# Softmax weights times values in float16 halves in the third and fourth token tile

## The chip, the cores and the metric

The kernel runs on one core of a Trainium2 chip. The metric is the device time of one execution in microseconds (us), lower is better. The kernel before takes 804.23 us, the median of 3 runs (804.05 to 804.49).

## The reference

```python
    x = A_x
    xn = _layernorm(x, axis=-1)
    s = _A_ref(xn, A_wqkv, A_wo)
    g = _silu(_B_ref(xn, B_w1, B_w3, B_w2))
    return x + s * g
...
        H = 32; Dh = D // H; W = 256
        qkv = (lambda x, *d: x.transpose(*d))((x @ wqkv).reshape(B, S, 3, H, Dh), 2, 0, 3, 1, 4)
        q, k, v = qkv[0], qkv[1], qkv[2]
        scores = jnp.einsum("bhqd,bhkd->bhqk", q, k) * (Dh ** -0.5)
        mask = (idx[:, None] - idx[None, :] >= 0) & (idx[:, None] - idx[None, :] < W)
        scores = jnp.where(mask[None, None], scores, -1e9)
        p = _softmax(scores, axis=-1)
        o = jnp.einsum("bhqk,bhkd->bhqd", p, v)
        return (lambda x, *d: x.transpose(*d))(o, 0, 2, 1, 3).reshape(B, S, D) @ wo
...
        gate = jnp.einsum("bsd,df->bsf", x, w1)
        up = jnp.einsum("bsd,df->bsf", x, w3)
        h = _silu(gate) * up
        out = jnp.einsum("bsf,fd->bsd", h, w2)
```

2048 tokens of 512 features go through a layernorm. Branch A is attention with 32 heads of 16 features, in which a token sees itself and the 255 tokens before it; branch B is a gated feed-forward layer of width 1792. All of it is in float32.

## The kernel before

**Halves.** Most products go through TensorE as float16: each operand is the sum of a high half (the number rounded to float16) and a low half (what the rounding left), and three products are summed: high times high, high times low, low times high. One product is an exception: the softmax weights times the values (L787) go through TensorE in float32, as one product.

**Tiles and units.** The 2048 tokens are cut into four token tiles of 512 (`t`, 0 to 3), the heads into four groups of eight (`g`). A unit is four of a group's eight heads in one token tile (`p`, 0 or 1): 32 units, numbered in order, so 16 to 31 belong to the third and fourth token tile. Each unit goes through two passes. `pass1` (L653) finds the maximum of each row of scores: eight pieces of matmuls (L671), each followed by two VectorE reductions with the window's mask (L685); then the maxima are negated (L704, L705), turned by a small matmul, copied (L717) and sent by DMA into rows of the query operand, so that the scores of pass 2 come out with the maximum subtracted. `pass2` (L738) computes the scores again, keys on the partitions, in five chunks of 128 x 1024 (L759); VectorE adds the masks (L766); ScalarE takes the exponential into a float32 tile `pt` (L769); and when all five are there, the values are multiplied in one burst (L787) of 48 float32 products, each of 64 rows (keys) by 32 columns (values of one head, with a column of ones that sums the weights), at eight places of the array. VectorE copies the result `po` out of PSUM (L802, L803), and units later it is normalised and multiplied by `wo`. While the chunks of a unit run, `pass1` of a later unit runs between them.

**Values.** `value(j)` (L553) projects the values of 128 tokens; ScalarE writes them with a scale to block `j % 10` of the tile `V`, float32, 17 columns for a head, the last of them ones.

**What else runs.** Between these pieces the dense products are spread: gate and up (L1055; ScalarE's sigmoid L1070, VectorE's products L1074 and L1079, and the casts and subtractions that make halves, L1110 to L1113), the projections of q and k (L601; L618 on ScalarE, L622 on VectorE), the folded down projection (L1198, L1280), and the output (L1332; L1326 on ScalarE, L1327 and L1336 on VectorE). L339 and L343 to L345 are helpers for the halves.

**Order.** Only TensorE runs in the order in which the code is written (`ORDERED`). That order comes from `batches`: a plan for each unit says which rows of work go into one batch, W being the scores of one chunk, M, X and N pieces of row maxima (X takes the bank `po`, N is narrow), the digits the chunks whose values are multiplied; `spread` lays dense work between the batches. The other engines are ordered by the scheduler of the language: each engine's instructions form one queue that is worked off in order, and `urgent()` puts an instruction ahead in it.

**Buffers.** PSUM has two banks `m` for dense results, two double banks `s` for scores and maxima, and one double bank `po`. SBUF has 54 slots (`take` and `give`) of 2 KB a partition; the exponentials have five buffers of their own (`pt`, from `ppool`).

```python
    PLAN = (("WM", ()), ("WMX", ()), ("WMX", ()), ("WWX", ()), ("NN", (0, 1, 2, 3, 4)))
```

## Time and profile before

| | |
|---|---|
| runs (3) | 804.23 us median, 804.05 to 804.49 |
| the profiled execution | 803.54 us, of which its span is 801.4 us |
| busy: TensorE, its weight loads | 791.6 us (99% of the span), 404.0 us (50%) |
| busy: VectorE, ScalarE, GpSimd | 620.4 us (77%), 395.5 us (49%), 387.6 us (48%) |
| clock granted to TensorE | full in every slice of the span |
| costliest on TensorE | L1055 first product 267.3 us in 896 instructions; L787 77.2 us in 2880 |
| costliest on VectorE | L685 133.9 us in 276 instructions out of `s` and 83.4 us in 172 out of `po`; L766 118.8 us in 280 |
| costliest on ScalarE | L769 167.6 us in 152 instructions |

A time of a group is the time in which at least one of its instructions ran, so groups whose instructions overlap share time. Busy is what the engine worked; the span is from the first to the last instruction, and 2.1 us of the execution lie around it. In the windows that follow, TensorE's clock, the share of the DMA engines and GB/s stand at the end of a row. In the timelines a row is the start, the duration, the engine, the line and operation, what it writes and reads, and in brackets how long the engine had been idle and what released it.

### The profile page before, as it was taken

How to read it: one execution, taken by the hardware profiler on the slowest of the kernel's cores; microseconds unless marked ns; L12 is line 12 of the kernel's file. 1: busy time of each engine (PE TensorE's matmuls, PEld its weight loads, DVE VectorE, ACT ScalarE, POOL GpSimd, SP SyncE). 2: the span in 40 equal slices, each digit the busy share in tenths (PEclk: the TensorE clock that was granted, in tenths of full speed). 3: DMA queues.
4: the chain of work that ended last, by engine and by line, in shares of the span. 5: the costliest groups of instructions: out<-in, count | busy, mean ns of one | idle time of the engine just before them, and what ended most of it. 6: DMA issues, size and time to landing. Idle time of an engine off the chain costs nothing.

```text
span 801.4 us, 23995 instructions
## 1 busy us (share of the span) xinstructions
PE 791.6 (99%) x9181; PEld 404.0 (50%) x9181; DVE 620.4 (77%) x2001; ACT 395.5 (49%) x596; POOL 387.6 (48%) x762
## 2 busy tenths in 40 slices
PE   9999999999999999999999999999999999999997
PEld 4444445444454444444445444466544744467465
DVE  8886889778798678787888887776678876874537
ACT  6989777744355544344443344344434334444411
POOL 2357657633329436365443546330446276650770
PEclk9999999999999999999999999999999999999999
DMA  9887655636666564657556743656553553343431
GB/s 284 239 260 239 202 185 145 242 111 193 189 216 187 168 212 139 212 156 255 142 191 171 209 115 101 180 169 159 140 158 90 156 161 106 89 121 127 133 89 60
DMA packets 109858, 134.18 MB, mean 167 GB/s; under 512 B 18928, under 2 KB 64944, under 8 KB 109744
## 3 DMA queue, kind: packets, MB, share of 16 engines
q1 hardware_dynamic: 109456, 132.13, 55.4%
q8 instruction: 72, 1.18, 0.7%
q10 hardware_dynamic: 288, 0.52, 0.2%
q14 instruction: 42, 0.34, 0.1%
HBM read 91.23 MB, written 36.57 MB: 159 GB/s over the span
## 4 chain that ended last, share of the span: by engine, by line
PE 81%; DVE 6%; DMA 5%; ACT 3%; SPq 3%; issue 1%; POOL 1%; DVEq 0%; ACTq 0%; POOLq 0%
PE m L1055 31%; PE po L787 9%; PE m L601 8%; PE m L1198 8%; PE m L1280 7%; PE s L759 5%; PE m L1332 4%; PE m L567 4%; PE s L671 3%; DMA slot<-in_B_w_dram 2%; PE po L671 2%; DVE junk L685 1%; POOL slot L345 1%; DMA KA<-dK 1%; SPq L880 1%
## 5 line engine op out<-in xcount | busy, mean ns | idle before, releaser
L1055 PE MATMUL m<-XH,slot 128*128 128x512 f16 x896 | 267.3, 380 | 0.8 <-DVE slot L1074 0.4
L769 ACT ACTIVATE pt<-s,es 128x1024 f32<-128x1024 f32 x152 | 167.6, 1113 | 175.9 <-DVE s L766 168.8
L1055 PEld LDWEIGHTS <-slot 128*128 128x128 f16 x1344 | 124.8, 98 | 155.2 <-issue 12.6
L1055 PE MATMUL m<-XL,slot 128*128 128x512 f16 x448 | 169.8, 379 | 0.0
L766 DVE TENSOR_TENSOR s<-s,MK 128x256 f32<-128x256 f32 (+2 forms) x280 | 118.8, 434 | 54.5 <-PE s L759 50.0
L685 DVE CUSTOM_DVE_ANT_0 junk<-s,MW 128x320 bf16<-128x320 f32 x276 | 133.9, 485 | 19.8 <-PE s L671 11.3
L339 POOL TENSOR_TENSOR slot<-slot,slot 128x256 f16<-128x256 f32 (+1 forms) x86 | 57.6, 693 | 121.4 <-DVE slot L1336 54.7
L345 POOL TENSOR_TENSOR slot<-slot,slot 128x128 f16<-128x128 f32 x184 | 74.9, 441 | 77.8 <-ACT slot L343 51.3
L685 DVE CUSTOM_DVE_ANT_0 junk<-po,MW 128x320 bf16<-128x320 f32 x172 | 83.4, 485 | 4.6
L1280 PE MATMUL m<-slot,slot 128*128 128x512 f16 x336 | 78.5, 380 | 1.4 <-DVE slot L1074 1.4
L787 PE MATMUL po<-pt,V 64*32 64x320 f32 (+4 forms) x2880 | 77.2, 342 | 0.1
L601 PE MATMUL m<-XH,slot 128*128 128x512 f16 x240 | 70.8, 380 | 0.5 <-DVE slot L1074 0.5
L1198 PE MATMUL m<-slot,slot 128*128 128x256 f16 x588 | 68.4, 273 | 0.0
L1070 ACT ACTIVATE slot<-m,sgs 128x512 f32<-128x512 f32 x56 | 38.3, 685 | 60.4 <-PE m L1055 60.3
L1113 POOL TENSOR_TENSOR slot<-slot,slot 128x256 f16<-128x256 f32 x98 | 64.6, 671 | 1.1
L1198 PEld LDWEIGHTS <-slot 128*128 128x128 f16 x588 | 56.2, 98 | 11.4 <-issue 2.8
L787 PEld LDWEIGHTS po<-pt,V 64*32 64x32 f32 x2880 | 50.5, 106 | 22.4 <-issue 0.8
L1074 DVE SCALAR_TENSOR_TENSOR slot<-slot,m 128x512 f32<-128x512 f32 x56 | 38.3, 684 | 28.4 <-ACT slot L1070 27.9
L759 PE MATMUL s<-qa,KA 50*64 50x320 f16 (+3 forms) x1472 | 58.3, 259 | 0.0
L601 PEld LDWEIGHTS <-slot 128*128 128x128 f16 x392 | 36.5, 98 | 42.6 <-issue 1.8
L759 PEld LDWEIGHTS <-KA 50*64 50x64 f16 x1472 | 30.1, 105 | 51.7 <-issue 31.5
L1280 PEld LDWEIGHTS <-slot 128*128 128x128 f16 x336 | 30.8, 98 | 39.5 <-issue 5.1
(194 smaller groups left out, 1132.6 us busy)
## 6 DMA issues: line engine op xcount, KB each, us to landing
slot<-dW SPq DMA_DIRECT2D x98, 256.0 KB
slot<-in_B_w_dram SPq DMA_DIRECT2D x56, 256.0 KB
slot<-dFold SPq DMA_DIRECT2D x48, 256.0 KB
dW<-slot SPq DMA_DIRECT2D x42, 256.0 KB
slot<-in_A_x_dram SPq DMA_DIRECT2D x30, 256.0 KB
KA<-dK SPq DMA_DIRECT2D x24, 288.0 KB
slot<-dWQ SPq DMA_DIRECT2D x24, 256.0 KB
qa<-dQ SPq DMA_DIRECT2D x30, 192.0 KB
```

The source lines that it names most:

```text
L339: op(out[:, c], a[:, c], b[:, c])
L345: nc.gpsimd.tensor_sub(lo[:, c:c + P], raw[:, c:c + P], hi[:, c:c + P])
L601: nc.tensor.matmul(cell["pp"][:, cols[n]], w[:, (a * NC + c) * P:(a * NC + c + 1) * P], b[:, c, cols[n]], start=n == 0 and (c, i) == parts ...
L685: lasts["maximum"] = nc.vector.tensor_tensor_reduce(out=junk[:, :n], in0=s[:, r, :n], in1=mask, scale=1.0, scalar=NEG, op0=ALU.add, op1=AL ...
L759: nc.tensor.matmul(s[64 * h:64 * h + 64, r, o:o + 64 * n], ka[rows, 2 * p + a, 64 * (m + 4):64 * (m + 5)], qa[rows, 2 * p + a, 64 * (m + k ...
L766: nc.vector.tensor_add(v, v, MK[:, kind, of:of + n, :].unsqueeze(1).to_broadcast([P, 2 * len(which), n, 64]))
L769: lasts["exp"] = nc.scalar.activation(pt, s, AF.Exp, scale=es)
L787: nc.tensor.matmul(cell["po"][32 * i:32 * i + 32, h, 64 * (m + k):64 * (m + k + n)], V[64 * h:64 * h + 64, (4 * t + m // 2) % VB, hd * VW: ...
L1055: nc.tensor.matmul(cell[k], w[:, (a * NC + c) * P:(a * NC + c + 1) * P], b[:, c, :], start=c == 0 and i == 0, stop=c == NC - 1 and i == 2)
L1113: nc.gpsimd.tensor_sub(lo, view, hi)
L1198: nc.tensor.matmul(cell["ps"][:, c], made[:, f:f + P], wj[:, g:g + 256], start=j == j0 and c == 0 and n == 0, stop=j == j1 - 1 and n == 2, ...
L1280: nc.tensor.matmul(ps, hh[:, a * TW + b * P:a * TW + (b + 1) * P], w[:, c * D:(c + 1) * D], start=f == f0 and i == 0, stop=f == f1 - 1 and ...
```

## The change

For the tiles `t` = 2 and 3 (units 16 to 31) the weights and the values become float16 halves, and the burst becomes three products of 48 matmuls each, 144 in all, in the order high weights by high values, high weights by low values, low weights by high values, within each group of pieces. The first two tiles keep the float32 product.

For each chunk of such a unit, the exponential (L790 now) is written to one of two float32 tiles, `pt0` and `pt1` in turn; ScalarE copies it to the high half (L801, 1024 columns); VectorE subtracts the high half from the second 512 columns (L802) and GpSimd from the first 512 in two pieces of 256 (L804). The halves of chunks 0 and 1 lie in slots, those of chunks 2, 3 and 4 in the buffers `pt2` to `pt4`. `urgent()` stands around all of these.

The values of blocks 8 to 15 are written as two halves (ScalarE the high one, a new VectorE operation the low one, four GpSimd memsets the columns of ones and the rest); blocks 6 and 7, which the second and the third tile read, are split by `part_values` at unit 13. The scale of the values becomes a constant, so two small scales that were computed at the start fall away. The plan of the two tiles is `PARTED_PLAN`: two chunks of scores in the first batch, in place of the fourth, and the first piece of maxima is in the second batch; units 30 and 31 keep `LAST_PLANS`. `parted` lets the matmul that turns the earlier unit's maxima go after the first piece of maxima of a unit.

```diff
--- before.py
+++ after.py
@@ -50,6 +50,8 @@
 TWO_ONES = struct.unpack("f", struct.pack("ee", ONE, ONE))[0]
 VW = DH + 1
 VB = 10
+VS = 2.0**8
+VR = H * VW + DH
 SLOTS = 54
 ORDERED = {ENGINE.PE}
 GROUPS = ((0, 4), (4, 8), (8, 11), (11, 14))
...
@@ -219,7 +222,9 @@
     for nm in NM:
         nc.gpsimd.memset(nm, 0.0)
 
-    V = const.tile([P, VB, H * VW + DH], F32, name="V")
+    V = const.tile([P, VB, VR], F32, name="V")
+    VF = {}
+    in_pt = [0]
     KA = [const.tile([P, 4, KW], F16, name=f"KA{r}") for r in range(3)]
     dQ = [dram.tile([P, TERMS, S], F16, name=f"dQ{g}") for g in range(NG)]
     dK = [dram.tile([P, TERMS, S], F16, name=f"dK{g}") for g in range(NG)]
@@ -565,10 +570,24 @@
             for c in (2 * half, 2 * half + 1):
                 for i, (a, b) in enumerate(((xh, WVH), (xh, WVL), (xl, WVH))):
                     nc.tensor.matmul(pv, a[:, c, tok], b[c], start=c == 0 and i == 0, stop=c == NC - 1 and i == 2)
-            if half:
+            if not half:
+                return
+            by_head = lambda v: v[:, 0:H * VW].rearrange("p (h w) -> p h w", w=VW)
+            pv = pv.rearrange("p (h d) -> p h d", d=DH)
+            s = VS / (WS * XS)
+            if j < 8:
                 with urgent():
-                    nc.scalar.activation(V[:, j % VB, 0:H * VW].rearrange("p (h w) -> p h w", w=VW)[:, :, 0:DH],
-                                         pv.rearrange("p (h d) -> p h d", d=DH), AF.Copy, scale=sc["uv"])
+                    nc.scalar.activation(by_head(V[:, j % VB, :])[:, :, 0:DH], pv, AF.Copy, scale=s)
+                return
+            both = V[:, j % VB, :].bitcast(F16)
+            VF[j] = hi, lo = both[:, 0:VR], both[:, VR:]
+            with urgent():
+                nc.scalar.activation(by_head(hi)[:, :, 0:DH], pv, AF.Copy, scale=s)
+                lasts["emptied"] = nc.vector.scalar_tensor_tensor(by_head(lo)[:, :, 0:DH], pv, s, by_head(hi)[:, :, 0:DH],
+                                                                  op0=ALU.mult, op1=ALU.subtract)
+            for v, one in ((hi, VS / OS), (lo, 0.0)):
+                nc.gpsimd.memset(by_head(v)[:, :, DH], one)
+                nc.gpsimd.memset(v[:, H * VW:], 0.0)
         return opening([(6, lambda h=h: part(h)) for h in range(2)])
 
 
@@ -673,12 +692,12 @@
             after = []
             if narrow:
                 pass
-            elif alone[0] and maxima and (ii, a) != (0, 0):
+            elif alone[0] and maxima and (parted[0] or (ii, a) != (0, 0)):
                 after = [f(s) for f in maxima]
                 maxima.clear()
             elif alone[0] and besides:
                 after = [besides.pop(0)(s)]
-            alone[0] = not after or t * NG + g <= 2
+            alone[0] = not after or t * NG + g <= 2 or parted[0]
             for r in range(2):
                 junk = ppool.tile([P, D], BF16, name="junk", bufs=1)
                 with urgent():
@@ -764,9 +783,25 @@
                 v = sv[:, :, first:first + by * (n - 1) + 1:by, :]
                 with urgent():
                     nc.vector.tensor_add(v, v, MK[:, kind, of:of + n, :].unsqueeze(1).to_broadcast([P, 2 * len(which), n, 64]))
-            cell[c] = pt = ppool.tile([P, 2, 512], F32, name="pt")
+            if t < 2:
+                in_pt[0] += 1
+            pt = ppool.tile([P, 2, 512], F32, name="pt", tag=f"pt{c % 2 if t > 1 else in_pt[0] % 5}", bufs=1)
             with urgent():
                 lasts["exp"] = nc.scalar.activation(pt, s, AF.Exp, scale=es)
+            if t < 2:
+                cell[c] = pt
+                return
+            if c < 2:
+                cell[c] = hi, lo = [take(F16) for _ in range(2)]
+            else:
+                both = ppool.tile([P, 2048], F16, name="pt", tag=f"pt{c}", bufs=1)
+                cell[c] = hi, lo = both[:, 0:1024], both[:, 1024:]
+            pt = pt.rearrange("p r q -> p (r q)")
+            with urgent():
+                lasts["exp"] = nc.scalar.copy(hi, pt)
+                nc.vector.tensor_sub(lo[:, 512:], pt[:, 512:], hi[:, 512:])
+                for q in (0, 256):
+                    nc.gpsimd.tensor_sub(lo[:, q:q + 256], pt[:, q:q + 256], hi[:, q:q + 256])
 
         begun = set()
 
@@ -779,7 +814,23 @@
                 for item in pieces(c):
                     if item[3][4]:
                         turns.setdefault(item[1:3], []).append((c, *item))
-            for group in zip_longest(*(turns[k] for k in sorted(turns))):
+            groups = list(zip_longest(*(turns[k] for k in sorted(turns))))
+            if t > 1:
+                for group in groups:
+                    for kv, kp in ((0, 0), (1, 0), (0, 1)):
+                        for c, o, h, a, (m, k, n, _, _) in filter(None, group):
+                            for r in range(2):
+                                i = 2 * r + a
+                                hd = g * 8 + r * 4 + 2 * p + a
+                                nc.tensor.matmul(cell["po"][32 * i:32 * i + 32, h, 64 * (m + k):64 * (m + k + n)],
+                                                 VF[4 * t + m // 2][kv][64 * h:64 * h + 64, hd * VW:hd * VW + 32],
+                                                 cell[c][kp][64 * h:64 * h + 64, 512 * r + o:512 * r + o + 64 * n],
+                                                 start=(h, i) not in begun, stop=c == len(chunks) - 1 and kp == 1,
+                                                 skip_group_check=True)
+                                begun.add((h, i))
+                give(*cell[0], *cell[1], after=2)
+                return
+            for group in groups:
                 for c, o, h, a, (m, k, n, _, _) in filter(None, group):
                     for r in range(2):
                         i = 2 * r + a
@@ -1469,6 +1520,7 @@
     FIRST_PLAN = (("WM", ()), ("WMX", ()), ("WMX", ()), ("WMX", ()), ("M", (0, 1, 2, 3)))
     PLAN = (("WM", ()), ("WMX", ()), ("WMX", ()), ("WWX", ()), ("NN", (0, 1, 2, 3, 4)))
     AHEAD_PLAN = (("MMX", ()), ("MMX", ()), ("MM", ()))
+    PARTED_PLAN = (("WW", ()), ("WMX", ()), ("WMX", ()), ("WMX", ()), ("NN", (0, 1, 2, 3, 4)))
     LAST_PLANS = ((("LW", ()), ("WW", ()), ("WW", ()), ("", (0, 1, 2, 3, 4))),
                   (("WW", ()), ("WW", ()), ("W", ()), ("", (0, 1, 2, 3, 4))))
 
@@ -1476,7 +1528,7 @@
 
         rows1 = pass1(*ahead) if ahead else []
         rows2, cols = pass2(*u) if u else ([], None)
-        plan = AHEAD_PLAN if not u else LAST_PLANS[n - len(units) + 2] if not ahead else PLAN if u[0] else FIRST_PLAN
+        plan = AHEAD_PLAN if not u else LAST_PLANS[n - len(units) + 2] if not ahead else (FIRST_PLAN, PLAN, PARTED_PLAN, PARTED_PLAN)[u[0]]
         made = []
         for kinds, cs in plan:
             rows = []
@@ -1490,6 +1542,7 @@
 
             def batch(rows=rows, cs=cs):
                 alone[0] = True
+                parted[0] = bool(u) and u[0] > 1
                 for f in rows:
                     f()
                 if cs:
@@ -1598,15 +1651,13 @@
     with tc.issue_after(lasts["hi"].ins), tc.issue_after(lasts["cut"].ins):
         wv[3]()
     run(k01[1:])
-    sc["uv"] = scaled(SQ["wv"][2], 1.0 / (WS * XS), "uv")
-    ones = scaled(SQ["wv"][2], 1.0 / OS, "ones")
     with tc.issue_after(lasts["hi"].ins), tc.issue_after(lasts["cut"].ins):
         measure(0)
     run(project(0, 1, 0, scores_bank=scores_bank))
     later(1, lambda: fetch(0, 1))
     run(value(0, True))
     nc.scalar.activation(V[:, :, 0:H * VW].rearrange("p b (h w) -> p b h w", w=VW)[:, :, :, DH],
-                         onesb[:, 0:H].unsqueeze(1).to_broadcast([P, VB, H]), AF.Copy, scale=ones)
+                         onesb[:, 0:H].unsqueeze(1).to_broadcast([P, VB, H]), AF.Copy, scale=VS / OS)
     qk[2][1]()
     run(value(1))
     qk[3][0]()
@@ -1623,6 +1674,16 @@
         nc.vector.tensor_scalar(us, SQ["wo"][2], SQ["wv"][2], 0.5 / (WS * OS), op0=ALU.mult, op1=ALU.mult)
         sc["y"] = us
 
+
+    def part_values():
+
+        for j in (6, 7):
+            VF[j] = hi, lo = [take(F16) for _ in range(2)]
+            with behind_exp():
+                nc.scalar.copy(hi[:, 0:VR], V[:, j, :])
+            for c in range(0, VR, 256):
+                cols = slice(c, min(c + 256, VR))
+                nc.gpsimd.tensor_sub(lo[:, cols], V[:, j, cols], hi[:, cols])
 
     beside = [[] for _ in units]
     ahead = [[] for _ in units]
@@ -1650,11 +1711,15 @@
         if n == 1:
             run(first[4:])
             second()
+        if n == 13:
+            later(2, part_values)
         if n == 6:
             wout[0]()
         if n == 7:
             wout[1](2)
             beside_scores(12, lambda s: then(s, wout[2](s), lambda: later(2, lambda: wout[3](2)), lambda: later(3, out_scale)))
+        if n == 24:
+            later(1, lambda: give(*VF.pop(6), *VF.pop(7)))
         want += a_unit - other[n]
         mine = more(want)
 
```

With the shift of lines, L766 is L785, L685 is L704, L802 and L803 are L853 and L854, L1055 is L1106, L1070, L1074 and L1079 are L1121, L1125 and L1130, L1110 is L1161, L618 and L622 are L637 and L641, and L1326, L1327 and L1336 are L1377, L1378 and L1387. Two places show what moves. In the order of VectorE, the start of unit 19, the fourth unit of the third tile, read before (`s` are scores or maxima in PSUM, `MK` and `MW` masks, `M` the maxima, `m0` and `m1` the dense banks; the short rows of L685 read a maximum out):

```order
L766 TENSOR_TENSOR s_8625<-s_8625,MK_119 128x4x2x64 [waits PE_49]
L1074 SCALAR_TENSOR_TENSOR slot46_8619<-slot46_8619,m1_8526 128x512 [waits Activation_49]
L685 ISA junk_8642,M_8624<-s_8637,MW_111 128x320 [waits PE_49]
L685 ISA M_8624 128x1
L685 ISA junk_8644,M_8624<-s_8637,MW_111 128x320 [waits DVE_49]
L685 ISA M_8624 128x1
L1079 SCALAR_TENSOR_TENSOR slot46_8619<-m0_8651,slot46_8619 128x512 [waits PE_49]
L766 TENSOR_TENSOR s_8686<-s_8686,MK_119 128x4x64 [waits PE_49,Activation_49]
L685 ISA junk_8706,M_8624<-s_8699,MW_111 128x320 [waits DVE_49,PE_49]
```

and now:

```order
L785 TENSOR_TENSOR s_9022<-s_9022,MK_119 128x4x2x64 [waits PE_49]
L1125 SCALAR_TENSOR_TENSOR slot32_9016<-slot32_9016,m1_8827 128x512 [waits Activation_49]
L785 TENSOR_TENSOR s_9040<-s_9040,MK_119 128x4x64 [waits PE_49]
L785 TENSOR_TENSOR s_9040<-s_9040,MK_119 128x2x2x64 [waits DVE_49]
L802 TENSOR_TENSOR slot44_9035<-pt_9032,slot50_9034 128x512 [waits Activation_49]
L1130 SCALAR_TENSOR_TENSOR slot32_9016<-m0_9064,slot32_9016 128x512 [waits PE_49]
L802 TENSOR_TENSOR slot18_9054<-pt_9051,slot25_9053 128x512 [waits Activation_49]
L785 TENSOR_TENSOR s_9099<-s_9099,MK_119 128x4x64 [waits PE_49]
L704 ISA junk_9124,M_9021<-s_9117,MW_111 128x320 [waits PE_49]
```

The masks of the second chunk have come ahead to the first chunk's, the first maxima have gone behind, and two subtractions that wait for ScalarE stand between them, one of them ahead of L1130.

In the order of ScalarE the same place read before:

```order
L1070 ACTIVATE slot46_8619<-m1_8526,sgs_155 128x512 [waits DMAHW1_49,PE_49]
L769 ACTIVATE pt_8635<-s_8625,es1_396 128x1024 [waits DVE_49,Activation_49]
L1110 CAST slot40_8674<-slot46_8619 128x256 [waits DVE_49]
L1110 CAST slot40_8674<-slot46_8619 128x256
L769 ACTIVATE pt_8697<-s_8686,es1_396 128x1024 [waits DVE_49,PE_49,Activation_49]
L618 ACTIVATE slot48_8736<-m1_8679 128x512 [waits DMAHW2_49,PE_49]
```

and now:

```order
L1121 ACTIVATE slot32_9016<-m1_8827,sgs_155 128x512 [waits DMAHW0_49,PE_49]
L790 ACTIVATE pt_9032<-s_9022,es1_396 128x1024 [waits DVE_49,Activation_49,Pool_49]
L801 CAST slot50_9034<-pt_9032 128x1024 [waits DMAHW2_49,DMAHW1_49,Activation_49]
L790 ACTIVATE pt_9051<-s_9040,es1_396 128x1024 [waits DVE_49,PE_49]
L801 CAST slot25_9053<-pt_9051 128x1024 [waits DMAHW3_49,Activation_49]
L1161 CAST slot2_9087<-slot32_9016 128x256 [waits DVE_49]
L1161 CAST slot2_9087<-slot32_9016 128x256
L790 ACTIVATE pt_9110<-s_9099,es1_396 128x1024 [waits DVE_49,PE_49,Pool_49]
L637 ACTIVATE slot9_9154<-m1_9092 128x512 [waits PE_49]
L801 CAST pt_9112<-pt_9110 128x1024 [waits Activation_49]
```

Behind each exponential stands its cast; the first exponential now waits for GpSimd too, which subtracts out of the `pt` tile that it takes over; and the third chunk's cast stands behind L637.

More of the change, by code (lines that the diff above doesn't have):

```diff
@@ L177, in tile_block @@
     alone = [True]
+    parted = [False]
     behind = []
```

## The prediction

> **What bounds the kernel now.** I read the page first (busy shares, chain), then the windows of the third and fourth token tile, then the timeline of one unit there. The page:
>
> ```profile
> span 801.4 us, 23995 instructions
> PE 791.6 (99%) x9181; PEld 404.0 (50%) x9181; DVE 620.4 (77%) x2001; ACT 395.5 (49%) x596; POOL 387.6 (48%) x762
> PE 81%; DVE 6%; DMA 5%; ACT 3%; SPq 3%; issue 1%; POOL 1%; DVEq 0%; ACTq 0%; POOLq 0%
> ```
>
> TensorE is busy for 99% and carries 81% of the chain. A unit is one pair of heads per half of a head group (32 in all, numbered from 0); 16 to 31 belong to the tiles that change. Windows show busy time of PE, PEld, DVE, ACT, POOL in this order. Below stand unit 14, then units 16 to 29 together, then unit 19 alone:
>
> ```profile
> 370.58:391.18 20.60, 20.60 (x259) 9.68 (x255) 19.69 (x66) 8.70 (x11) 10.49 (x18) 1.00 0.73 213
> 413.33:725.87 312.54, 312.29 (x3984) 166.10 (x3981) 242.44 (x751) 126.07 (x163) 149.90 (x254) 1.00 0.50 141
> 481.91:503.43 21.52, 21.45 (x262) 10.03 (x258) 17.07 (x54) 8.95 (x12) 13.20 (x24) 1.00 0.44 119
> ```
>
> In the fourteen units TensorE has no gap (312.3 of 312.5 us; 22.3 a unit). VectorE is at 242.4, or 17.3 a unit: a second queue not far behind. Its own timeline in unit 19 tells how far:
>
> ```profile
> 483.14 0.69 DVE L802 COPY os<-po 128x512 f32<-128x512 f32 x1
> 484.47 0.69 DVE L766 TENSOR_TENSOR s<-s,MK 128x512 f32<-128x512 f32 x1
> 485.07 0.68 DVE L1074 SCALAR_TENSOR_TENSOR slot<-slot,m 128x512 f32<-128x512 f32 x1
> 485.67 0.48 DVE L685 CUSTOM_DVE_ANT_0 junk<-s,MW 128x320 bf16<-128x320 f32 x1
> 486.61 0.69 DVE L1079 SCALAR_TENSOR_TENSOR slot<-m,slot 128x512 f32<-128x512 f32 x1
> 488.32 0.43 DVE L766 TENSOR_TENSOR s<-s,MK 128x256 f32<-128x256 f32 x1 [1.02 <-PE s L759]
> 491.25 0.69 DVE L622 SCALAR_TENSOR_TENSOR slot<-m,slot 128x512 f16<-128x512 f32 x1 [0.18 <-ACT slot L618]
> 492.89 0.43 DVE L766 TENSOR_TENSOR s<-s,MK 128x256 f32<-128x256 f32 x1 [0.95 <-PE s L759]
> 495.35 0.49 DVE L685 CUSTOM_DVE_ANT_0 junk<-po,MW 128x320 bf16<-128x320 f32 x1
> 495.88 0.49 DVE L685 CUSTOM_DVE_ANT_0 junk<-po,MW 128x320 bf16<-128x320 f32 x1
> 496.90 1.41 DVE L766 TENSOR_TENSOR s<-s,MK 128x256 f32<-128x256 f32 x4
> 500.77 0.69 DVE L1327 SCALAR_TENSOR_TENSOR slot<-slot,slot 128x512 f32<-128x512 f32 x1 [1.52 <-ACT slot L1326]
> 504.96 0.69 DVE L802 COPY os<-po 128x512 f32<-128x512 f32 x1
> ```
>
> From one L802 copy to the next are 21.82 us. The waits in brackets sum to 3.67, some smaller gaps to 0.3: 17.85 us of work without waiting. Back to back, a 512-column operation holds VectorE 0.60 (484.47 to 485.07 to 485.67), a maximum with its readout 0.53 (495.35 to 495.88), a 256-column mask 0.34 (1.41 for four that overlap).
>
> **The value products on TensorE.** A burst before, and what stands around it:
>
> ```profile
> 495.73 0.64 PE L759 MATMUL s<-qa,KA 50*64 50x320 f16 x24
> 496.44 0.33 PE L671 MATMUL po<-KA,qa 48*64 48x320 f16 x4
> 500.69 0.47 PE L671 MATMUL s<-KA,qa 48*32 48x320 f16 x16
> 500.97 2.53 PE L787 MATMUL po<-pt,V 64*32 64x256 f32 x96
> 503.44 0.61 PE L1055 MATMUL m<-XH,slot 128*128 128x512 f16 x2
> 511.26 0.38 PE L567 MATMUL m<-wvh,XH 128*128 128x512 f16 x1
> 511.47 0.38 PE L567 MATMUL m<-wvl,XH 128*128 128x512 f16 x1
> ```
>
> The float32 burst holds TensorE 2.47 us (500.97 to 503.44). The code's pieces give each of the eight positions 20 x 64 = 1280 columns. A float16 column takes 0.21/512 = 0.42 ns (511.26 to 511.47), so three products take at least 3 x 1280 x 0.42 = 1.6 us. Above: 24 L759 products took 0.71, 30 ns each, and 144 at that rate 4.3 us. The nearer row is L671, which uses the same eight positions: 16 in 0.28, or 17.5 ns, which is what its 640 columns a position cost (0.27), so issue had not yet bound it. I take 1.9: the column time and 0.3 for the two of six groups whose pieces are 64 or 128 columns. **Gain 0.5 a unit, 8 us in 16 units**; bounds -0.9 and +1.8 a unit.
>
> The Trainium skill (TensorE: Matmul & The Clock Gate, "Wait — 56ns, not 53.3ns?") says that starts never come closer than about 25 ns, however few the columns. By that rule a burst would be 3.6 us and TensorE 18 us slower in all; the 17.5 ns of the trace speak against it where products go to different positions.
>
> **VectorE and the new wait.** Each unit's five chunks add a ScalarE cast of 1024 columns, a VectorE subtraction of 512 and two GpSimd subtractions of 256. The rows nearest to them, for ScalarE also the exponential, and what the masks release:
>
> ```profile
> L854 DVE TENSOR_TENSOR slot<-on,slot x1: 681/681/681, 783.6 to 783.6; 128x512 f16<-128x512 f32 x1
> L343 ACT CAST slot<-slot 128x512 f16<-128x512 f32 x46 | 27.4, 610 | 0.5
> L1110 ACT CAST slot<-slot 128x256 f16<-128x256 f32 x42 | 15.6, 403 | 59.8 <-DVE slot L1079 59.8
> L769 ACT ACTIVATE pt<-s,es 128x1024 f32<-128x1024 f32 x152 | 167.6, 1113 | 175.9 <-DVE s L766 168.8
> L1113 POOL TENSOR_TENSOR slot<-slot,slot 128x256 f16<-128x256 f32 x98 | 64.6, 671 | 1.1
> 506.29 0.69 DVE L766 TENSOR_TENSOR s<-s,MK 128x512 f32<-128x512 f32 x1
> 507.08 1.11 ACT L769 ACTIVATE pt<-s,es 128x1024 f32<-128x1024 f32 x1 [1.45 <-DVE s L766]
> ```
>
> L854 is the same form as the new subtraction: 0.68 long, 0.60 of VectorE's time; five make **3.0 us**. The cast grows by 0.21 per 256 columns, so 1024 take 1.02. From a mask's end a subtraction is then ready after 0.10 (506.98 to 507.08) + 1.11 + 1.02, about 2.2 us; and VectorE takes its queue in order. In unit 19 its queue starts so (s tiles are the scores of chunks 0 and 1, L802 the subtractions):
>
> ```order
> L785 TENSOR_TENSOR s_9022<-s_9022,MK_119 128x4x2x64 [waits PE_49]
> L1125 SCALAR_TENSOR_TENSOR slot32_9016<-slot32_9016,m1_8827 128x512 [waits Activation_49]
> L785 TENSOR_TENSOR s_9040<-s_9040,MK_119 128x4x64 [waits PE_49]
> L785 TENSOR_TENSOR s_9040<-s_9040,MK_119 128x2x2x64 [waits DVE_49]
> L802 TENSOR_TENSOR slot44_9035<-pt_9032,slot50_9034 128x512 [waits Activation_49]
> L1130 SCALAR_TENSOR_TENSOR slot32_9016<-m0_9064,slot32_9016 128x512 [waits PE_49]
> L802 TENSOR_TENSOR slot18_9054<-pt_9051,slot25_9053 128x512 [waits Activation_49]
> ```
>
> Between the first mask's end and its L802 stand 0.60 + 2 x 0.34 = 1.3 us of work: VectorE stands for 1.0. The second chunk's exponential and cast follow on ScalarE, some 1.95 later; subtraction and L1130 fill 1.2 of that: 0.75 more. Chunk 2 waits 0.3 behind L637's ScalarE work; chunk 3 has four maxima and L1130 ahead, and no wait. Chunk 4:
>
> ```order
> L785 TENSOR_TENSOR s_9251<-s_9251,MK_119 128x2x2x64 [waits DVE_49]
> L704 ISA junk_9280,M_9021<-s_9273,MW_111 128x320 [waits DVE_49]
> L704 ISA junk_9287,M_9021<-po_9282,MW_111 128x320 [waits DVE_49,PE_49]
> L704 ISA junk_9289,M_9021<-po_9282,MW_111 128x320 [waits DVE_49]
> L802 TENSOR_TENSOR pt_9268<-pt_9266,pt_9268 128x512 [waits Activation_49,Pool_49]
> L1378 SCALAR_TENSOR_TENSOR slot6_9292<-slot6_9292,slot1_4981 128x512 [waits Activation_49]
> ```
>
> Three maxima are 1.5 us, so 0.75. Together 2.8 us in which what is queued behind (L1130 and L1378 with L1387, which empty TensorE's m banks, and L704, which frees s and po) comes late, and TensorE waits for those banks. So VectorE needs 17.85 + 3.0 + 2.8 = 23.6 us for unit 19, against 21.8 now. Over the fourteen units: 17.3 busy + 0.8 of small gaps + 3.0 = 21.1, and waits between 0 (everything else ready in their places) and 2.8. I take 2.5, since busier units put more between mask and subtraction: 23.6 against 22.3, **+1.3 x 14 = +18 us**. TensorE's saving vanishes there; units 30 and 31, without maxima, keep it: -1.
>
> **The rest.** Eight value tiles get a VectorE operation more, 0.60 each; four fall in units 12 to 15, where unit 14 has 0.9 us left of 20.6: +0.5 once; four in units 20 to 23 (+0.2 a unit over fourteen, inside the waits taken). GpSimd gets 10 x 0.67 = 6.7 on 10.7 a unit: 17.4 of 23.6, hidden, 6.7 if not. Its memsets, the splitting of values 6 and 7, and the constants in place of two scales are hidden by the same slack of GpSimd and ScalarE (8.7 of 20.6); uncovered, some 4 us once. PARTED_PLAN moves chunk scores and row maxima between batches and adds none. Sum: +18 - 1 + 0.5 = +17.5. The profiled execution took 803.54 us (2.1 around its span), 0.7 below the runs' median: 803.5 + 17.5 = 821, and by the median 822.
>
> **GpSimd beside VectorE.** Both subtract at the same moment, out of SBUF:
>
> ```profile
> 701.42 1.24 POOL L1112 CAST slot<-slot 128x256 f16<-128x256 f32 x2
> 701.71 0.69 DVE L1327 SCALAR_TENSOR_TENSOR slot<-slot,slot 128x512 f32<-128x512 f32 x1 [1.44 <-ACT slot L1326]
> 512.61 0.74 POOL L1112 CAST slot<-slot 128x256 f16<-128x256 f32 x2
> 571.10 1.41 POOL L339 TENSOR_TENSOR on<-on,rb 128x256 f32<-128x256 f32 x2 [22.55 <-DMA qa<-dQ]
> ```
>
> Beside L1327 two casts took 1.24 instead of 0.74; L1327 kept its 0.69. So GpSimd's half comes 0.5 late, and VectorE's does not: no charge. The Trainium skill (SBUF — State Buffer, "Who interferes with whom") says that an operation of VectorE with two SBUF inputs and a reading GpSimd operation shut each other out, and that the first to issue wins. By it VectorE could also lose up to 0.67 a subtraction; here the row shows GpSimd as the one that pays.
>
> **Rivals.** (1) TensorE stays the bound and the change is **faster**: the waits for ScalarE fall where VectorE waits for TensorE now (3.67 us in unit 19). It decides when they cost VectorE under 0.7 a unit (21.1 + 0.7 = 21.8). For it: unit 14 runs VectorE at 19.69 of 20.60 with no gap on TensorE. Against: a late VectorE finds TensorE's results ready, and its ScalarE waits remain. -0.5 x 16: 796 us. (2) Both cancel, with waits near 1.3 a unit: 804. (3) Issue binds the burst at 4.3 us: TensorE needs 22.3 + 1.8 = 24.1 a unit, +1.8 x 16: 833. The L671 rate speaks against it. (4) GpSimd is late: a subtraction behind L339 (above, 22.55 us idle for a DMA) keeps its pt buffer, and the next exponential but one waits with all of ScalarE's queue. That wait ended 1.1 us into unit 23, so mostly before the first subtraction; 4 us in four of the units on top of the forecast: 838.
>
> **How the numbers follow.** Forecast 0.61, rival 1 0.13, rival 2 0.05, rival 3 0.08, rival 4 0.13. The likeliest: 822, by its own bounds 806 (waits 1.5) to 830. For 8 in 10 the range leaves out rival 1 and the top: 803 to 838. Beyond 0.2% (1.6 us, what a measurement of this kernel tells from none): faster 0.13, same 0.05, slower 0.82.
>
> **What would show it.** A burst of 144 near 1.9 us; VectorE near 287 us busy over units 16 to 29 and L802 idle for ScalarE some 30 us; TensorE with 20 us or more of gaps there, ended by VectorE or ScalarE. I am wrong if TensorE stays without gaps (rival 1), a burst exceeds 3 us (3), or L802's idle time is under 10 us.

## The result, and the profile after

The changed kernel takes 888.51 us (median of 4 runs, 888.24 to 891.34) against 804.22 us: 1.1056 times as long, 95% interval 1.1033 to 1.1078. The forecast was 822, so the direction was right and the size nearly five times too small: +84 instead of +18.

Three lines of the page of the changed kernel; the last gives the shares of the chain of work that ended last:

```profile
span 886.5 us, 25972 instructions
PE 811.6 (92%) x9949; PEld 413.7 (47%) x9949; DVE 702.1 (79%) x2087; ACT 471.2 (53%) x678; POOL 531.8 (60%) x960
PE 9%; POOL 9%; DVE 6%; ACT 4%; issue 3%; SPq 1%; DMA 1%; DVEq 0%; ACTq 0%; POOLq 0%
```

TensorE fell from 99% to 92% of a longer span, and no engine has taken its place: VectorE has 79%, ScalarE 53%, GpSimd 60%. The chain could be followed back only to 596.5 us, so its shares sum to a third; in that part GpSimd stands level with TensorE, 9% each, where before, over the whole span, it had 1% and TensorE 81%. The windows from the burst of unit 16 to that of unit 29, which hold thirteen units (17 to 29), of the changed kernel:

```profile
442.18:795.44 353.26, 306.73 (x4277) 162.27 (x4253) 285.07 (x753) 177.23 (x215) 247.61 (x361) 0.95 0.39 113
```

and of the kernel before:

```profile
433.90:723.41 289.51, 289.26 (x3701) 154.90 (x3684) 222.04 (x692) 116.93 (x151) 137.64 (x233) 1.00 0.50 140
```

A unit went from 22.27 to 27.17 us, so 63.8 of the 85.1 us of span lie here. Most of the rest is at both ends: 7.1 between the bursts of units 15 and 16, and 10.7 between those of units 29 and 31, where the forecast had a gain of 1. Of the 63.8 us, 46.3 are gaps of TensorE (46.5, against 0.3 before) and 17.5 longer busy time of TensorE, whose granted clock fell to 0.95. Per unit VectorE is busy for 21.9 us and idle for 5.2. What TensorE waits for, from the first changed unit on, by the view of waits (total, times, longest):

```profile
PE po L825 <- POOL pt L804: 18.3, 11, 4.1
PE s L690 <- ACT pt L790: 7.6, 11, 2.2
PE m L1106 <- DVE slot L1125: 7.4, 4, 3.9
PE s L778 <- DVE M L704: 7.0, 10, 1.4
PE po L690 <- DVE XL L530: 5.7, 4, 2.9
PE m L620 <- DVE slot L1130: 2.8, 1, 2.8
```

It waits for three engines in turn: for GpSimd's halves in the middle of a burst, for exponentials and maxima that free `s`, for VectorE's products (L1125, L1130) that free `m`. VectorE's costliest groups in the thirteen units show the new operation:

```profile
L802 DVE TENSOR_TENSOR pt<-pt 128x512 f16<-128x512 f32 x38 | 38.7, 1018 | 20.5 <-ACT pt L801 20.4
L802 DVE TENSOR_TENSOR slot<-pt,slot 128x512 f16<-128x512 f32 x26 | 26.2, 1012 | 25.1 <-ACT slot L801 24.9
```

It takes 1.01 us, not the 0.68 of L854, and VectorE stands 45.3 us for ScalarE's cast ahead of it, 3.5 a unit. The timelines of one chunk, the fourth of unit 20, in the order of the work:

```profile
541.03 0.42 DVE L785 TENSOR_TENSOR s<-s,MK 128x256 f32<-128x256 f32 x1
541.56 1.11 ACT L790 ACTIVATE pt<-s,es 128x1024 f32<-128x1024 f32 x1 [2.58 <-DVE s L785]
542.71 1.04 ACT L801 CAST pt<-pt 128x1024 f16<-128x1024 f32 x1
543.83 1.75 POOL L804 TENSOR_TENSOR pt<-pt 128x256 f16<-128x256 f32 x2 [0.94 <-ACT pt L801]
543.86 1.19 DVE L802 TENSOR_TENSOR pt<-pt 128x512 f16<-128x512 f32 x1 [0.83 <-ACT pt L801]
```

From the mask's start to the last half are 4.55 us through four instructions in a row on three engines; with one product in float32 the chunk would have been ready at the exponential's end, after 1.64. GpSimd began 0.03 us ahead of VectorE: its first piece took its usual time, L802 stood until it was over (1.19 instead of 0.69), and the second piece stood behind L802. The other meetings go by this pattern: of the 80 L802 in the trace, the 15 that began with no GpSimd operation running took 0.68 to 0.69 us, though one started beside each of them and most of those took 1.17 to 1.19 instead of 0.67; the 65 that began while GpSimd was running took 1.05 on average.

### The profile page after: what moved, and what is told of

It reads as the page before. It is cut to its first block, busy times and chain, and to the rows that moved or that the text cites. A ratio compares the mean times of both kernels' runs of the same rounds, so it can differ in the third digit from the quotient of the medians.

```text
span 886.5 us, 25972 instructions
## 1 busy us (share of the span) xinstructions
PE 811.6 (92%) x9949; PEld 413.7 (47%) x9949; DVE 702.1 (79%) x2087; ACT 471.2 (53%) x678; POOL 531.8 (60%) x960
## 5 line engine op out<-in xcount | busy, mean ns | idle before, releaser
L1106 PE MATMUL m<-XH,slot 128*128 128x512 f16 x896 | 274.1, 388 | 10.6 <-DVE slot L1125 7.4
L790 ACT ACTIVATE pt<-s,es 128x1024 f32<-128x1024 f32 x152 | 167.8, 1113 | 213.9 <-DVE s L785 161.0
L1106 PEld LDWEIGHTS <-slot 128*128 128x128 f16 x1344 | 127.4, 99 | 170.1 <-issue 30.3
L1106 PE MATMUL m<-XL,slot 128*128 128x512 f16 x448 | 173.5, 387 | 0.0
L704 DVE CUSTOM_DVE_ANT_0 junk<-s,MW 128x320 bf16<-128x320 f32 x276 | 133.4, 483 | 14.5 <-PE s L690 7.2
L785 DVE TENSOR_TENSOR s<-s,MK 128x256 f32<-128x256 f32 (+2 forms) x280 | 119.4, 434 | 17.4 <-PE s L778 14.3
L804 POOL TENSOR_TENSOR pt<-pt 128x256 f16<-128x256 f32 x96 | 77.7, 832 | 50.2 <-ACT pt L801 40.2
L344 POOL TENSOR_TENSOR slot<-slot,slot 128x256 f16<-128x256 f32 (+1 forms) x86 | 58.0, 697 | 52.6 <-ACT slot L1139 42.0
L704 DVE CUSTOM_DVE_ANT_0 junk<-po,MW 128x320 bf16<-128x320 f32 x172 | 83.7, 486 | 6.3
L620 PE MATMUL m<-XH,slot 128*128 128x512 f16 x240 | 72.9, 390 | 4.6 <-DVE slot L1130 2.8
L802 DVE TENSOR_TENSOR pt<-pt 128x512 f16<-128x512 f32 x48 | 47.0, 980 | 32.0 <-ACT pt L801 31.9
L1164 POOL TENSOR_TENSOR slot<-slot,slot 128x256 f16<-128x256 f32 x98 | 71.5, 744 | 1.0
L804 POOL TENSOR_TENSOR slot<-pt,slot 128x256 f16<-128x256 f32 x64 | 48.9, 789 | 35.9 <-ACT slot L801 35.9
L778 PE MATMUL s<-qa,KA 50*64 50x320 f16 (+3 forms) x1472 | 60.3, 263 | 8.0 <-DVE M L704 7.0
L1121 ACT ACTIVATE slot<-m,sgs 128x512 f32<-128x512 f32 x56 | 38.4, 686 | 52.4 <-PE m L1106 52.3
L1249 PEld LDWEIGHTS <-slot 128*128 128x128 f16 x588 | 56.2, 98 | 12.6 <-issue 3.7
L778 PEld LDWEIGHTS <-KA 50*64 50x64 f16 x1472 | 32.1, 107 | 62.5 <-issue 27.1
L620 PEld LDWEIGHTS <-slot 128*128 128x128 f16 x392 | 37.1, 99 | 49.0 <-issue 9.0
L802 DVE TENSOR_TENSOR slot<-pt,slot 128x512 f16<-128x512 f32 x32 | 31.4, 983 | 32.9 <-ACT slot L801 32.7
```

The lines of the kernel that those rows point to most:

```text
L620: nc.tensor.matmul(cell["pp"][:, cols[n]], w[:, (a * NC + c) * P:(a * NC + c + 1) * P], b[:, c, cols[n]], start=n == 0 and (c, i) == parts ...
L704: lasts["maximum"] = nc.vector.tensor_tensor_reduce(out=junk[:, :n], in0=s[:, r, :n], in1=mask, scale=1.0, scalar=NEG, op0=ALU.add, op1=AL ...
L778: nc.tensor.matmul(s[64 * h:64 * h + 64, r, o:o + 64 * n], ka[rows, 2 * p + a, 64 * (m + 4):64 * (m + 5)], qa[rows, 2 * p + a, 64 * (m + k ...
L785: nc.vector.tensor_add(v, v, MK[:, kind, of:of + n, :].unsqueeze(1).to_broadcast([P, 2 * len(which), n, 64]))
L790: lasts["exp"] = nc.scalar.activation(pt, s, AF.Exp, scale=es)
L802: nc.vector.tensor_sub(lo[:, 512:], pt[:, 512:], hi[:, 512:])
```

## The experiments

Four theories of the missing 66 us were set up, A to D in the texts below. Each kernel ran once unless said otherwise, beside runs of the kernel before that took 803.7 to 804.9 us, so differences of 2 or 3 us say little. E1 to e4 take the parts away one at a time. The diffs are shown in part.

**E1, no subtraction.**

```diff
-                cell[c] = hi, lo = both[:, 0:1024], both[:, 1024:]
+                hi = both[:, 0:1024]
+                cell[c] = hi, hi
...
-                nc.vector.tensor_sub(lo[:, 512:], pt[:, 512:], hi[:, 512:])
-                for q in (0, 256):
-                    nc.gpsimd.tensor_sub(lo[:, q:q + 256], pt[:, q:q + 256], hi[:, q:q + 256])
```

> Leaves out every subtraction of the weights: the third product uses the high halves again, so VectorE and GpSimd get nothing new per chunk; the cast, the 144 products and the plan stay. Two theories of the lost time: A, VectorE and GpSimd hold each other up while both subtract (L802 took 1.00 us on average in units 17 to 29 where the forecast had 0.60); B, VectorE stands in its queue for ScalarE's cast (64.6 us idle before L802); C, GpSimd's half comes late, and the burst and the exponentials wait for it (18.3 and 25.9 us). All three expect this run at TensorE's own time: 804 minus 0.5 us for each of 16 units, 794 to 800 us, with no gaps on TensorE in units 17 to 29. If it is above 815, the cast, the burst or the plan cost more than thought, and none of the three is enough.

Measured: 821.7 us. Without a single new instruction on VectorE or GpSimd per chunk, the kernel is 17 us slower than before. All three theories missed, and the forecast too, which had costed the cast at nothing.

**E2, VectorE's half alone, and e3, GpSimd's half alone.** E2 leaves out GpSimd's two pieces and its index is `kp * r`; e3's edit is below:

```diff
-                nc.vector.tensor_sub(lo[:, 512:], pt[:, 512:], hi[:, 512:])
...
-                                                 cell[c][kp][64 * h:64 * h + 64, 512 * r + o:512 * r + o + 64 * n],
+                                                 cell[c][kp * (1 - r)][64 * h:64 * h + 64, 512 * r + o:512 * r + o + 64 * n],
```

> Leaves out GpSimd's half: for the two heads of the first 512 columns the third product uses the high half again; VectorE subtracts its 512 columns as in the changed kernel. B (VectorE's wait for the cast) expects nearly all of the loss here: 870 to 888 us, L802 idle for ScalarE still near 4 us a unit. A and C expect the forecast's sum, since only VectorE's 3.0 us of work and some wait are left: 810 to 830 us, with L802 at 0.68 us each.

> Leaves out VectorE's half instead: for the two heads of the last 512 columns the third product uses the high half; GpSimd subtracts its two pieces of 256 columns per chunk. C (GpSimd late by itself) expects a good part of the loss: 840 to 888 us, with TensorE waiting for L804 as before (18 us or more). A expects little, because GpSimd meets no subtraction on VectorE: 796 to 810 us, with the pieces near 0.67 us. B expects 796 to 800 us.

Measured: e2 848.6, e3 843.9. Each half costs by itself, 26.9 and 22.2 us over e1; B's and A's numbers both fell. C's time came for e3, but TensorE waits there for GpSimd for 9.7 us and not the 18 that C named, and C can't explain e2. Both halves together cost 66.8, 17.7 more than the sum. The waits of e3, on TensorE and on ScalarE (L803 is GpSimd's half there):

```profile
PE po L824 <- POOL pt L803: 9.7, 7, 3.4
ACT pt L790 <- POOL slot L803: 13.4, 6, 4.1
```

Between the bursts of units 16 and 30 of e3 GpSimd was busy for 230 of 342.5 us, two thirds, and was late all the same: its pieces stand in one queue with the dense work's halves. Ahead of the longest of these waits of TensorE (3.4 us, until 683.46) GpSimd's pauses add up to 0.2 us in the last 7.

**E4, the plan alone** (with `parted`), on the kernel before.

```diff
+    PARTED_PLAN = (("WW", ()), ("WMX", ()), ("WMX", ()), ("WMX", ()), ("NN", (0, 1, 2, 3, 4)))
```

> The kernel before with the new plan of the third and fourth tile alone (float32 products, no halves). All theories: the plan moves the same work between batches, 802 to 807 us. If it is above 812, the plan is part of the loss.

Measured: 806.3, against 804.7 beside it, so the plan is no part of the loss worth naming.

**E5, no cast.**

```diff
-                lasts["exp"] = nc.scalar.copy(hi, pt)
+                lasts["exp"] = nc.scalar.activation(hi.rearrange("p (r q) -> p r q", r=2), s, AF.Exp, scale=es)
```

> Leaves out the subtractions and the cast: the exponential writes the high half itself, and the third product uses the high halves again; 144 products and the plan stay. Run e1 (without subtractions) took 821.7 us, 15.4 more than the plan alone (806.3) though its bursts are 0.5 us shorter in 16 units. D, that ScalarE's cast makes this, because it stands in ScalarE's queue ahead of the sigmoid of L1121 and the next exponential, expects 806.3 - 8 = 796 to 800 us here. The rival, that the new bursts, the halves of the values or the buffers make it, expects 815 us or more.

Measured: 803.3, just past D's 796 to 800 and far from its rival's 815. The cast with its float32 buffers is worth 18.4 us; the bursts bring 3.0 against the plan alone, hardly more than single runs differ by, and not the 8 that 16 x 0.5 promised. Where the rest of it went was not followed.

**E6, all on GpSimd; e7, all on VectorE; e8, GpSimd copies.** The edit is e7's; in e6 GpSimd takes four pieces of 256 columns, in e8 its two pieces are copies of the high half.

```diff
+                nc.vector.tensor_sub(lo, pt, hi)
```

> All of the subtraction on GpSimd, four pieces of 256 columns per chunk; VectorE has none. A (the two engines hold each other up): VectorE has no subtraction to be held up, GpSimd's pieces stay near 0.7 us, and the time falls to 860 us or less. B (VectorE's wait in its queue): as A, since the wait is gone. C (GpSimd late): 10.7 + 20 x 0.67 = 24.1 us of GpSimd a unit and halves that come 2.7 us after the cast instead of 1.35, so TensorE and the exponentials wait longer for it than in e3 (843.9): 865 to 900 us.

> All of the subtraction on VectorE, one operation of 1024 columns per chunk; GpSimd has none. A: no subtraction meets another, so 860 us or less, with the operation near 1.2 us. B: e2 with its 512 columns took 848.6; 512 columns more are 0.53 us of VectorE, five a unit, 16 units: 848.6 + 42 = 890 us, since VectorE had only some 4 us idle a unit, all of it waiting for the cast. C: 848.6 to 860 us, since nothing waits for GpSimd.

> As the changed kernel, but GpSimd's pieces copy the high half instead of subtracting (one input instead of two; the low half of the first 512 columns holds the high half again); VectorE's half, all waits and buffers stay. A: L802 falls from 1.00 to below 0.80 us, and the time from 888 to 850 to 865 us. B and C: L802 may fall, but the time stays above 870 us, apart from what GpSimd saves by shorter pieces.

Measured: e6 905.3, e7 873.8, e8 866.2. E6 is just past C's range, and TensorE stands 39.4 us in its bursts for GpSimd's halves; e7 falls between A and B, and past C's 860; e8 is faster by 22.3, just above A's range and below the 870 of B and C. L802 in e8, where GpSimd's pieces take 0.40 us and read one tile:

```profile
L802 DVE TENSOR_TENSOR pt<-pt 128x512 f16<-128x512 f32 x48 | 36.9, 769 | 27.6 <-ACT pt L801 27.6
L802 DVE TENSOR_TENSOR slot<-pt,slot 128x512 f16<-128x512 f32 x32 | 27.6, 862 | 32.2 <-ACT slot L801 31.5 <-POOL slot L804 0.6
```

E8 changes more than its expectation says. A copy reads the high half and not the float32 tile `pt`, so no exponential waits for GpSimd to let go of it: these waits were 25.9 us in the changed kernel, and there are none in e8. Part of the 22.3 us can be theirs.

**E9, the subtraction later in VectorE's queue.**

```diff
...
+            def cut(lo=lo, pt=pt, hi=hi):
+                with tc.issue_after(lasts["mask"].ins):
+                    nc.vector.tensor_sub(lo[:, 512:], pt[:, 512:], hi[:, 512:])
+            pend.append(cut)
...
```

> The whole computation of the changed kernel; only VectorE's subtraction of a chunk moves in its queue, behind the masks of the next chunk (the first of a unit and the fifth stay where they were). B expects that the 64.6 us in which VectorE stands for the cast fall below 30, and the time from 888 to 840 to 860 us. A and C expect the idle time to fall but the time to stay at 870 to 888 us, since subtractions still meet and GpSimd's half is no earlier.

Measured: 867.8, 20.7 less, between B's range (840 to 860) and that of A and C (870 to 888). The waits of VectorE ahead of the subtraction (L810 here):

```profile
DVE slot L810 <- ACT slot L804: 23.3, 15, 2.4
DVE pt L810 <- ACT pt L804: 8.7, 10, 4.6
```

So 64.6 us of waiting became 32.0, near B's 30, and two thirds of that came out at the end. B is a real part, and not the whole.

**E10, the cast on GpSimd, without subtractions.**

```diff
+                for q in range(0, 1024, 256):
+                    nc.gpsimd.tensor_copy(hi[:, q:q + 256], pt[:, q:q + 256])
```

> As e1 (no subtractions, third product with the high halves), but GpSimd makes the cast, in four pieces of 256 columns (0.40 us each by L1163), and ScalarE only the exponential. D (the cast stands in ScalarE's queue ahead of the sigmoid and the next exponential) expects the 803.3 us of e5 within 4 us. The rival, that the later halves or the two float32 buffers make the 18.4 us of the cast, expects 815 us or more, since on GpSimd a cast takes 1.6 us instead of 1.04.

Measured: 834.6, against D's number. It doesn't clear D's rival, since GpSimd brought a wait of its own, 16.4 us of TensorE in the bursts and 30.9 us of exponentials for a float32 buffer. E13 tests D without that.

**E11, two products**, with weights rounded to float16 and the plan of before.

```diff
-                    for kv, kp in ((0, 0), (1, 0), (0, 1)):
+                    for kv in (0, 1):
```

> As e5 (the exponential writes the high half itself), with two products of 48 matmuls, high weights by the two halves of the values, and the plan of the kernel before; the low halves of the weights are left out, so the weights are rounded to float16. E5 took 803.3 us with bursts of 2.00 us. If TensorE sets the time, 48 matmuls fewer are 0.67 us a unit less, 10.7 us in 16 units, and the old plan 1.6: 789 to 795 us. If VectorE sets it by now, 798 to 803 us.

Measured: 791.16 us (median of 4 runs, 790.49 to 792.08), 0.9837 of the kernel before (0.9821 to 0.9854), inside the first range: with nothing new on the way to the matmul, TensorE sets the time. It is faster than both kernels, and less exact, since the low halves of the weights are missing.

**E12, GpSimd's copies without VectorE's half, and e13, a spare cast.** The edit is e13's.

```diff
+                lasts["exp"] = nc.scalar.activation(hi.rearrange("p (r q) -> p r q", r=2), s, AF.Exp, scale=es)
+                nc.scalar.copy(lo, hi)
```

> As e8 (GpSimd copies the high half into its half of the low half), but VectorE's half is left out, the third product using the high half there: the fourth corner of a square with e1 (neither, 821.7), e2 (VectorE alone, 848.6) and e8 (both, 866.2). With subtractions on GpSimd the square was 821.7, 848.6, e3 843.9 and 888.5: both together cost 17.7 us more than the sum of each alone. A (two-input operations shut each other out) expects that the copies, with one input, add no such excess: e12 at 866.2 - 26.9 = 839 us, within 4. If the excess comes from waits that stack up, whatever GpSimd does, e12 is at 825 us or less.

> As e5 (the exponential writes the high half itself, 803.3 us), but ScalarE also copies that half to a place that nothing reads: 1024 columns per chunk, as long as the cast if it costs the same. The matmuls don't wait for it and no float32 buffer is in the way; only ScalarE's queue is longer. D (the length of ScalarE's queue makes the cast's 18.4 us) expects 815 to 822 us. The rival (the halves come later, or the exponential waits for one of only two float32 buffers) expects 803 to 807 us.

Measured: e12 830.6, between the two numbers. With copies the excess of both over the sum of each is 866.2 - 848.6 - 830.6 + 821.7 = 8.7 us, with subtractions 17.7. About half of the excess goes when copies take the place of subtractions. Their shorter pieces of one input and the waits for `pt`, which copies don't cause, were not told apart, since no run gives the exponentials a third float32 buffer; whether the rest is the copies' own meetings with L802 or waits that stack up stays open too. E13 took 815.2: the spare copy is as long as the cast,

```profile
L803 ACT COPY pt<-pt x48: 1033/1045/1053, 425.0 to 775.0; 128x1024 f16<-128x1024 f16 x48
```

so 11.9 of the cast's 18.4 us are the longer queue of ScalarE, as D said. The product that frees `m` (L1125 in the changed kernel) stands behind the sigmoid in that queue, and TensorE's waits for it in e5, e13 and e1 show what came late:

```profile
PE m L1104 <- DVE slot L1123: 0.4, 1, 0.4
PE m L1105 <- DVE slot L1124: 5.9, 5, 2.3
PE m L1105 <- DVE slot L1124: 6.8, 5, 2.3
```

The other 6.5 come with the cast between exponential and matmul or the float32 buffers, which were not told apart.

The steps from 806.3 (plan) to 888.5, from one run each:

| part | runs | us |
|---|---|---|
| shorter bursts, halves of the values | e5 - e4 | -3.0 |
| ScalarE's queue longer | e13 - e5 | +11.9 |
| cast on the way to the matmul | e1 - e13 | +6.5 |
| VectorE's half | e2 - e1 | +26.9 |
| GpSimd's half | e3 - e1 | +22.2 |
| both at once | | +17.7 |

## Why the prediction was wrong

**The burst: right.** Forecast 1.9 us for 144 products; 2.00 in a burst that nothing held up, out of 2.53 before. Rival 3 (4.3 us by issue) didn't come. Its sign did, a burst over 3 us, in nine of the sixteen units, but each of the nine waited for GpSimd's halves in the middle, and in e1, without them, thirteen of the sixteen take 2.00. The chain of e1 has 132 records of one burst in 1.81 us:

```profile
438.73 1.81 PE po L824 x132
```

That is 13.7 ns for one. The floor of about 25 ns that the Trainium skill gives (TensorE: Matmul & The Clock Gate, "Wait — 56ns, not 53.3ns?") doesn't hold for products at different places of the array.

**VectorE's half: right in kind, too small.** The step took work of 3.0 and waits of 2.5 us a unit. E2 shows VectorE's half alone at +26.9 us in all, against +17.5 forecast for everything. In the changed kernel the waits were 3.5 a unit and the five L802 took 5.0. In units 16 to 29 VectorE was busy for 311.9 us where near 287 were named, and L802 stood 48.7 us for ScalarE where some 30 were (64.6 in all). A reading of rival 1 was off too: of the 3.67 us in unit 19 in which it has VectorE wait for TensorE, 1.70 are waits for ScalarE.

**"So GpSimd's half comes 0.5 late, and VectorE's does not: no charge": wrong.** In the row it rested on, GpSimd's first cast was nearly over when L1327 began, and the second, which took the delay, started 0.05 us behind L1327; it showed who had come first, and was read as who yields. Here GpSimd mostly comes first. L802 took 78.4 us in the 80 chunks and 61.7 in e2, so with GpSimd's half in the other queue VectorE loses 16.7 us. That this is much like the 17.7 of excess doesn't make them one: in e8 L802 took 64.5 us, 2.8 more than in e2, and 8.7 of excess were left. The Trainium skill's rule (SBUF — State Buffer, "Who interferes with whom"), that the first to issue holds the other off, agrees with 1.19 against 0.69 above, and should have carried the weight. A queue of GpSimd work can hold VectorE off several times over, though in this trace it does so once in 80, and a waiting L802 mostly gets its turn after one operation; the timelines of unit 25, VectorE, GpSimd, TensorE:

```profile
663.35 4.43 DVE L802 TENSOR_TENSOR slot<-pt,slot 128x512 f16<-128x512 f32 x1 [0.95 <-ACT slot L801]
667.70 0.68 DVE L1130 SCALAR_TENSOR_TENSOR slot<-m,slot 128x512 f32<-128x512 f32 x1
...
661.99 1.41 POOL L344 TENSOR_TENSOR on<-on,rb 128x256 f32<-128x256 f32 x2
663.36 0.67 POOL L1164 TENSOR_TENSOR slot<-slot,slot 128x256 f16<-128x256 f32 x1
663.98 0.74 POOL L908 CAST slot<-on 128x256 f16<-128x256 f32 x2
664.68 1.30 POOL L344 TENSOR_TENSOR slot<-on,slot 128x256 f16<-128x256 f32 x2
665.94 1.29 POOL L804 TENSOR_TENSOR slot<-pt,slot 128x256 f16<-128x256 f32 x2
...
668.43 1.01 PE L620 MATMUL m<-XH,slot 128*128 128x512 f16 x2 [2.79 <-DVE slot L1130]
```

GpSimd was still at L344 when L802 began and had no pause in the seven operations behind it, and VectorE waited for all of them; L1130 behind it came late, and TensorE stood for 2.79 us.

**GpSimd's half "hidden", and the cast at nothing: the main error.** The sum has GpSimd's half as "17.4 of 23.6, hidden", and no term at all for the cast. The cast was taken into the 2.2 us until a subtraction is ready, but no step asked what the longer queue of ScalarE does to the next exponential and to L1121, or what GpSimd's half does to the burst. E1 against e5 and e3 against e1 put 18.4 and 22.2 us on these two, which the sum had at nothing; with the 17.7 of both halves at once they are 58 of the 66 us that the forecast missed. The idle time that the busy shares show (ScalarE busy for 8.7 of 20.6, GpSimd for 10.7 of 22.3) was no cover, because these engines are often not idle when the chunk comes. For the same reason the sum by one engine's demand was the wrong tool: between the bursts of units 16 and 30 VectorE is busy for 16.8 us a unit in e1 and in e3 alike, and a unit took 23.0 and 24.5, against 22.1 before. In the changed kernel its work and its wait for the cast come to 25.4 of 27.2, so there VectorE is near its limit; e1 and e3 lose their time without that.

**Rival 4** (GpSimd late) had the right place, at 16 us on top. The DMA that it named as the cause is behind two of the waits of the changed kernel's exponentials, 3.1 and 1.3 us in units 19 and 23; the longest of the others (5.0, 3.4 and 3.4 us) stand behind GpSimd's own queue, as in e3. **Units 30 and 31** were to keep the saving and lost 10.7 us: TensorE stood 7.3 us there for L1125. Ahead of the longest of these waits (3.9 us) its sigmoid stood behind two exponentials and two casts on ScalarE, and L1125 behind two L802.

## What to carry to other kernels

An operation put between two engines that hand work on was paid here in delay, on each queue that it lengthened, though every one of them had idle time; ask what stands behind it and when its result is needed. Where two engines are to share an operation out of the same memory, look in a trace for pairs in both orders of start before saying who pays. When no queue is full after a change and all are slower, price the parts one by one and in pairs: here the two halves together cost 17.7 us more than the sum of each alone.

## What the hardware showed besides

TensorE's granted clock was 1.00 throughout before and 0.95 in units 17 to 29 after, down to 0.88 in unit 25. After the gap of 2.79 us above the next products took twice as long for 4.6 us: those of 512 columns started 0.43 us apart instead of 0.21. There are nine such stretches, eight of them behind gaps of 2.0 us or more. The Trainium skill (TensorE: Matmul & The Clock Gate, "HAM oscillation — how this bites in real kernels") asks for no idle gap over some 3.4 us; here gaps of 2.0 to 2.9 were enough six times (the other two are of 3.9 and 4.1), though others of 2.5 were not followed by it. So a stall in this kernel costs more than its own length: the products of 512 columns in the two dense lines L1106 and L620 are busy for some 14 us longer than before for the same work:

```profile
L1106 PE MATMUL m<-XH,slot 128*128 128x512 f16 x459 | 143.8, 396 | 9.7 <-DVE slot L1125 7.4 <-DVE slot L641 1.9 <-DVE V L586 0.3
L1106 PE MATMUL m<-XL,slot 128*128 128x512 f16 x230 | 90.9, 395 | 0.0
```

(396 ns against 380 before.) The experiments show it too: the granted clock was 1.00 in e5, 0.978 after, and 0.96 in e6, the slowest.
